# Strassen's method for the first product of the first layer's last eight columns, in a kernel that runs attention and two feed-forward layers

## The chip, the cores and the metric

The kernel runs on one core of a Trainium2 chip. The metric is the device time of one execution in microseconds; the median of a few runs is compared. One execution was also profiled, and every row below is from that one.

## The reference, cut to what matters

```python
def _moe_ref(x, w_in, w_out):            # first layer
    h = x @ w_in
    g = np.maximum(h, 0.0) + np.log1p(np.exp(-np.abs(h)))      # softplus
    return g @ w_out

def _moe2_ref(x, w_in, w_out):           # second layer
    h = np.maximum(x @ w_in, 0.0)
    return h * h @ w_out

attn_out = _attn_ref(q, k, v)            # windowed attention plus block summaries
x = attn_out, as [1536 tokens, 512]
x = _moe_ref(x, moe_w_in, moe_w_out)     # w_in [512, 2048], w_out [2048, 512]
return _moe2_ref(x, moe2_w_in, moe2_w_out)
```

The weights come as 64-bit floats and are converted in the kernel. All else is float32.

## The kernel before, in words

**Arithmetic.** Each float32 operand of the two layers is split into a high and a low part, and a product is three matmuls: high by high, high by low, low by high. d_ff has 2048 units, worked on as 16 "columns" of 128.

**First layer.** Part A runs columns 0 to 3 on blocks of 256 tokens while the attention still produces tokens (`steps`, flag `A`). Part B runs columns 4 to 9 and then 10 to 15 on three blocks of 512 tokens each, 36 steps in all. A B step is 12 matmuls of 512 columns in `mlp_in` (L680), softplus and the split of the gate (L686, L687, L689), and 12 matmuls of 512 in `mlp_out` (L706). The outputs add up in four PSUM banks (`accp` is one tile of two banks) and go into `part` (L729).

**Second layer.** `second` takes two columns at a time (a pair) and two pairs of token blocks z of 768 tokens (2 x 384). Its first product is Strassen's method in Winograd's form: 7 products of 6 matmuls of 384 columns (L992) in place of 8. One pair with one z is a "quad"; there are 16. The sums of weight blocks are made on POOL (L921), the sums of token blocks on DVE (L885) and split on ACT and DVE (L876) in `prepare`. `gate` turns a block of the product into a gate: `keep` (ACT), `add` (L999), square (L1008), high part (ACT), low part (L1016). The second product is plain: 6 groups of 6 matmuls of 512 (L1063). On PE the products of one quad alternate with the output groups of the quad before.

**Weights.** A load (L620, L623) lands in one of the `raw` buffers (4 in part A, 3 in the second layer). Four passes make float32 of it: L630 (ACT), L635 (DVE), a scaling (L314, ACT), L635 (DVE). Then ACT copies the high part into a weight slot and POOL subtracts (L606, L935, L948). A raw buffer is held until that split is done, and the split waits until the slot is free. There are 9 slots.

**Order.** Every step is an operation in a planner (`Plan`) with engine, assumed duration, due time and dependencies. For each engine it fixes one order ahead of time: of the operations that its model finds ready, the one due first. On the chip each engine then works through its own list in order. `rel` keeps a load's conversion from starting more than HOLD = 100 us before it is due.

Of the kernel before, what the change touches and what calls it, by code (L numbers as in the profile page):

```python
# [22 lines left out]
PH = ((0, 4), (4, 10), (10, 16))  # L23
LAG = 2
QT = 15.44
FIRST = 12.72
LAG_A = 3
NW_A = 6
NW = 9
NRAW = 4  # L30
NG = 3
LEAD = 16.0
HOLD = 100.0
# [154 lines left out]
def kernel(  # L188
# [47 lines left out]
    ga = [[wr.tile([128, 512], F32R, name=f"g{i}{n}") for n in "hl"] for i in range(2)]  # L236
# [4 lines left out]
    ws = [slot(wr, i) for i in range(NW_A)]  # L241
# [4 lines left out]
    att = ExitStack()  # L246
# [39 lines left out]
    for L in (1,):  # L286
        for ph, (f0, f1) in enumerate(PH):
            A = L == 1 and ph == 0
            n = 256 if A else 512
            for t0 in range(0, NT, n):  # L290
                for f in range(f0, f1):
                    steps.append(dict(A=A, L=L, ph=ph, c=NF * (L - 1) + f, t0=t0, n=n, first=f == f0, last=f == f1 - 1,
                                      fin=ph == len(PH) - 1, lastblk=t0 + n == NT, g=len(steps)))
    T = 24.0
    due_c, due_b = {}, {}
    for st in steps:
        st["T"] = T
        due_c.setdefault(st["c"], T)
        if st["A"]:
            due_b.setdefault(st["t0"] // 256, T)  # L300
        T += 24 * 0.2267 * st["n"] / 512 + (13.0 / PH[0][1] if st["A"] and st["t0"] < 1024 else 0.0)

    def due_t(t):
        return due_b[t // 2] - LEAD - 13.0 + 6.5 * (t % 2)

    NA = sum(st["A"] for st in steps)

# [282 lines left out]
    def weight(c, which):  # L590
        f, wi, wo = c, w1_in, w1_out
        i, s = nwt[0] % NRAW, c % NW
        nwt[0] += 1
        due = due_c[c] + which * (4.0 if c < PH[0][1] else 8.0)
        dv, dl = due - DV, due - DL
        if c < EARLY:
# [3 lines left out]
        need = [] if s < NW_A else ["late places"]  # L600

# [3 lines left out]
           r=[RL] + need, w=[("w", s, kh)])  # L605
        op(("POOL", "DVE"), (1.4, 1.0), dv, lambda e: tt(e).tensor_tensor(  # L606
            out=ws[s][kl], in0=lo.bitcast(F32), in1=ws[s][kh].bitcast(F32), op=ALU.subtract),
            r=[RL, ("w", s, kh)] + need, w=[("w", s, kl)])
# [35 lines left out]
    g_t, tmp = [], []  # L644

    def places(st):

        i = st["g"] - NA
        if st["A"]:
            return i % 2, i % 4  # L650
        return i % 4, (i + 2) % NG

    def hview(st):
        return hb[places(st)[0]][:, 0:st["n"]]

    def gview(st):
        i = places(st)[1]
        if st["A"]:
            return [x[:, 256 * (i % 2):256 * (i % 2) + 256] for x in ga[i // 2]]
        return g_t[i]  # L660

    def gkeys(st):
        i = places(st)[1]
        return [("g", i // 2, i % 2)] if st["A"] else [("g", i, 0), ("g", i, 1)]

    def xkeys(st, n):
        return [(n, t) for t in range(st["t0"] // 128, (st["t0"] + st["n"]) // 128)]

    def mlp_in(st):
        due, n, s = st["T"], st["n"], st["c"] % NW  # L670
        bl, o = divmod(st["t0"], 512)
        H_ = ("h", places(st)[0])
        gk = [(*x, "h") for x in gkeys(st)], [(*x, "l") for x in gkeys(st)]
        need = [] if st["A"] else ["late places"]

        def mm(ks_):
            for kk in ks_:
# [5 lines left out]
        op("PE", 12 * (0.0105 + 0.2162 * f), due, lambda: mm(range(NK)),  # L683
           r=xkeys(st, "xh") + xkeys(st, "xl") + [("w", s, "ih"), ("w", s, "il")] + need, w=[H_])
        ta, tv = 0.2 + 0.4 * f, 0.14 + 0.55 * f
        op("ACT", ta, due, lambda: nc.scalar.activation(out=hview(st), in_=hview(st), func=AF.Softplus), w=[H_], tab="sp")  # L686
        op("ACT", ta, due, lambda: nc.scalar.activation(out=gview(st)[0], in_=hview(st), func=AF.Copy),  # L687
           r=[H_] + need, w=gk[0])
        op("DVE", tv, due, lambda: nc.vector.tensor_tensor(  # L689
            out=gview(st)[1], in0=hview(st), in1=gview(st)[0].bitcast(F32), op=ALU.subtract),  # L690
            r=[H_] + gk[0] + need, w=gk[1])

    def mlp_out(st, due, gap=0.0):
        n, s = st["n"], st["c"] % NW
        gk = [(*x, p) for x in gkeys(st) for p in "hl"]
        A = st["A"]

        def mm(ms):
            gh, gl = gview(st)
            oh, ol = ws[s]["oh"], ws[s]["ol"]  # L700
            prs = ((oh, gh), (ol, gh), (oh, gl))
            for m, c in [(m, c) for m in ms for c in range(3)] if A else [(m, c) for c in range(3) for m in ms]:
                sl = slice(128 * m, 128 * m + 128)
                o = acc[m // 2][:, 256 * (m % 2):256 * (m % 2) + 256] if A else acc[m]
                for a, b in (prs[c],):
                    nc.tensor.matmul(out=o, lhsT=a[:, sl], rhs=b,  # L706
                                     start=(st["first"] and c == 0 and not (A and m % 2)),
                                     stop=(st["last"] and c == 2 and not (A and m % 2 == 0)))
        for i in range(2):
            op("PE", 0.71 if A else 1.36, due + gap * i, lambda i=i: mm((2 * i, 2 * i + 1)),  # L710
               r=gk + [("w", s, "oh"), ("w", s, "ol")] + ([] if A else ["late places"]),
               w=[("acc", i)] if A else [("acc", 2 * i), ("acc", 2 * i + 1)])

    def evac(st, due):
        t0, n = st["t0"], st["n"]
        bl, o = divmod(t0, 512)
# [6 lines left out]
        for m in range(4):  # L723
            pt, k_ = part[bl][:, m], ("part", bl, m)
            if st["ph"] == 0:
                op("ACT", 0.6, due, lambda m=m, pt=pt: nc.scalar.activation(out=pt, in_=acc[m], func=AF.Copy),
                   r=[("acc", m)], w=[k_])
            else:
                op("DVE", 0.7, due, lambda m=m, pt=pt: nc.vector.tensor_tensor(out=pt, in0=acc[m], in1=pt, op=ALU.add),  # L729
                   r=[("acc", m)], w=[k_])  # L730
# [13 lines left out]
    def late_places():  # L744
# [4 lines left out]
        ws.extend(slot(wr2, i) for i in range(NW_A, NW))  # L749
        g_t.extend(ga)  # L750
        g_t.extend([wr2.tile([128, 512], F32R, name=f"g{i}{n}") for n in "hl"] for i in range(2, NG))
# [457 lines left out]
```

## Time and profile before

| what | us |
|---|---|
| median of 3 runs | 606.68 (605.65 to 607.19) |
| the profiled execution | 607.07 |
| its span in the trace | 605.4 |

The 1.67 us between the last two lie outside the traced program. In the page, "busy" of PE counts pipelined matmuls and overstates the work; the time from one matmul's start to the next one's is the safer measure. A chain of waits is followed back from the last instruction to what released each one.

### The profile page before, as it was taken

To read this page: it belongs to the slowest core of one execution; us is meant where nothing else is said; L and a number is where in the kernel's file an instruction comes from. 1 tells how busy PE (TensorE), PEld (TensorE's weight loads), DVE (VectorE), ACT (ScalarE), POOL (GpSimd) and SP (SyncE) were. 2 spreads that over 40 slices of the span, in tenths; PEclk is the share of its full clock that TensorE was granted. 3 is DMA by queue.
4 is the path that set the end of the run, shared out by engine and by line. 5 is a ranking of instruction groups with operands and counts; after the bars stand their busy time and mean duration, and the time that the engine had idled before them with its cause. 6 is when DMAs were issued, how large, how long until landed. Compare 5 with 4: busy or idle time off the path is not lost.

```text
span 605.4 us, 9947 instructions
## 1 busy us (share of the span) xinstructions
PE 586.3 (97%) x3905; PEld 512.6 (85%) x3905; DVE 396.6 (66%) x581; ACT 330.9 (55%) x599; POOL 247.6 (41%) x235
## 2 busy tenths in 40 slices
PE   8688999999999999999999999999999999999997
PEld 6577988999888888888888898899988888898896
DVE  4987999924665126350228389876868586877854
ACT  4776888865664226452135565685755454545330
POOL 5967697524651034530000451735616061615210
PEclk9998999999999999999999999999999999999999
DMA  8999732332542023120000421133212122222212
GB/s 274 244 283 222 178 86 54 87 93 83 169 140 74 0 71 104 57 83 2 0 1 0 140 69 36 66 109 100 74 54 73 50 71 69 70 69 70 97 43 104
DMA packets 67215, 55.56 MB, mean 92 GB/s; under 512 B 36448, under 2 KB 61024, under 8 KB 67168
## 3 DMA queue, kind: packets, MB, share of 16 engines
q1 hardware_dynamic: 67168, 54.93, 31.9%
q8 instruction: 30, 0.49, 0.4%
q14 instruction: 17, 0.14, 0.1%
HBM read 51.77 MB, written 3.15 MB: 91 GB/s over the span
## 4 chain that ended last, share of the span: by engine, by line
PE 76%; DVE 12%; DMA 5%; ACT 2%; POOL 1%; issue 1%; SPq 1%; ACTq 0%; POOLq 0%
PE h L680 19%; PE h L992 16%; PE accp L706 12%; PE acc L706 8%; PE h L1063 7%; PE acc L1063 7%; PE accp L1063 6%; DMA raw<-in_moe_w_in_dram 3%; DVE raw L635 2%; DMA vwin<-in_v_dram 2%; DVE sm L524 1%; DVE mx L538 1%; DVE s L507 1%; SPq L390 1%; PE ab L569 1%
## 5 line engine op out<-in xcount | busy, mean ns | idle before, releaser
L635 DVE SCALAR_TENSOR_TENSOR raw<-raw 128x512 uint32<-128x512 uint32 x144 | 118.0, 837 | 43.1 <-ACT raw L630 25.0
L680 PE MATMUL h<-x,wih 128*128 128x512 f32 (+1 forms) x480 | 125.4, 349 | 0.0
L680 PEld LDWEIGHTS h<-x,wih 128*128 128x128 f32 x480 | 83.7, 189 | 12.1 <-POOL raw L316 0.4
L686 ACT ACTIVATE h<-h 128x512 f32<-128x512 f32 (+1 forms) x60 | 29.8, 498 | 99.9 <-PE h L680 99.8
L680 PE MATMUL h<-x,wil 128*128 128x512 f32 (+1 forms) x240 | 83.1, 346 | 0.0
L630 ACT ACTIVATE raw<-raw 128x512 uint32<-128x512 uint16 x67 | 44.8, 671 | 18.4 <-DMA raw<-in_moe_w_in_dram 9.4
L948 POOL TENSOR_TENSOR wil<-raw,wih 128x512 fp32r<-128x512 f32 x10 | 14.6, 1457 | 87.8 <-ACT wih L314 72.0
L680 PEld LDWEIGHTS h<-x,wil 128*128 128x128 f32 x240 | 45.3, 189 | 5.5
L314 ACT ACTIVATE raw<-raw 128x512 f32<-128x512 f32 x57 | 38.2, 672 | 17.9 <-DVE raw L635 17.9
L935 POOL TENSOR_TENSOR wih<-raw,wih 128x512 fp32r<-128x512 f32 x10 | 14.9, 1489 | 77.1 <-ACT wih L314 77.1
L921 POOL TENSOR_TENSOR raw<-raw 128x256 f32<-128x256 f32 x30 | 28.3, 945 | 29.6 <-DVE raw L635 29.1
L992 PE MATMUL h<-x,wil 128*128 128x384 f32 x192 | 38.5, 336 | 0.0
L992 PEld LDWEIGHTS h<-x,wil 128*128 128x128 f32 x192 | 34.4, 188 | 2.7
L992 PE MATMUL h<-x,wih 128*128 128x384 f32 x192 | 35.9, 335 | 0.0
L992 PEld LDWEIGHTS h<-x,wih 128*128 128x128 f32 x192 | 33.8, 188 | 1.4
L689 DVE TENSOR_TENSOR g1l<-h,g1h 128x256 fp32r<-128x256 f32 (+1 forms) x24 | 13.2, 550 | 26.3 <-ACT g1h L687 26.2
L314 ACT ACTIVATE woh<-raw 128x512 fp32r<-128x512 f32 (+1 forms) x34 | 22.2, 654 | 14.1 <-DVE raw L1008 6.0
L999 DVE TENSOR_TENSOR t<-t,h 128x384 f32<-128x384 f32 x32 | 17.6, 550 | 18.0 <-ACT t L314 12.3
L992 PE MATMUL h<-x,woh 128*128 128x384 f32 x144 | 28.9, 335 | 0.0
L316 POOL TENSOR_SCALAR wih<-raw 128x512 fp32r<-128x512 f32 x10 | 7.4, 736 | 52.5 <-PE h L680 44.8
L544 POOL TENSOR_TENSOR s<-s,sm 128x960 f32<-128x960 f32 (+1 forms) x14 | 22.5, 1610 | 13.4 <-DVE sm L526 12.5
L314 ACT ACTIVATE t<-h 128x384 f32<-128x384 f32 x32 | 15.6, 487 | 21.8 <-PE h L992 21.8
(343 smaller groups left out, 1551.2 us busy)
## 6 DMA issues: line engine op xcount, KB each, us to landing
raw<-in_moe_w_in_dram SPq DMA_DIRECT2D x36, 512.0 KB, 4.0
raw<-in_moe_w_out_dram SPq DMA_DIRECT2D x36, 512.0 KB, 3.3
vwin<-in_v_dram SPq DMA_DIRECT2D x20, 192.0 KB, 5.6
part<-in_k_dram SPq DMA_DIRECT2D x12, 256.0 KB, 5.5
late<-in_v_dram SPq DMA_DIRECT2D x2, 1536.0 KB, 11.2
out_dram<-part SPq DMA_DIRECT2D x12, 256.0 KB, 2.0
part<-in_q_dram SPq DMA_DIRECT2D x10, 256.0 KB, 5.3
vwin<-in_v_dram SPq DMA_DIRECT2D x4, 160.0 KB, 5.1
```

The source lines that it names most:

```text
L314: nc.scalar.activation(out=out_, in_=in_, func=AF.Copy, **({} if mul is None else {"scale": mul}))
L544: op(("POOL", "DVE"), (1.8 * n + 0.1, 1.75 * n), due, lambda e, sv=sv, rv=rv, spread=spread: tt(e).tensor_tensor(out=sv, in0=sv, in1=sprea ...
L630: nc.scalar.activation(out=lo, in_=q4[:, :, 1], func=AF.Copy, scale=2.0 ** -13, bias=-4095.5 / 8192.0)
L635: nc.vector.scalar_tensor_tensor(out=lo, in0=hi, scalar=n, in1=lo, op0=how, op1=ALU.bitwise_or)
L680: nc.tensor.matmul(out=hview(st), lhsT=ws[s][wn][:, w_], rhs=xx[bl][:, kk, o:o + n], start=(kk == 0 and xx is xh and wn == "ih"), stop=(kk ...
L686: op("ACT", ta, due, lambda: nc.scalar.activation(out=hview(st), in_=hview(st), func=AF.Softplus), w=[H_], tab="sp")
L706: nc.tensor.matmul(out=o, lhsT=a[:, sl], rhs=b, start=(st["first"] and c == 0 and not (A and m % 2)), stop=(st["last"] and c == 2 and not ...
L921: op("POOL", 0.85, due - 5.0 + d, lambda: nc.gpsimd.tensor_tensor(out=to, in0=x, in1=y, op=o), r=r, w=w)
L935: op("POOL", 0.2 + 1.2 * n / 512, d, lambda o=o_, j=j, x=x: nc.gpsimd.tensor_tensor(out=o(4 + j), in0=x, in1=o(j).bitcast(F32), op=ALU.sub ...
L992: nc.tensor.matmul(out=bk(b), lhsT=ws[i][m][:, c], rhs=half((z, x, xp), kk), start=first and kk == 0 and n == 0, stop=kk == 1 and n == 2, ...
L999: op("DVE", 0.58, URG, lambda: nc.vector.tensor_tensor(out=tmp[to], in0=tmp[x], in1=bk(b), op=ALU.add), r=[kb_(b)] + ([kt(x)] if x != to e ...
L1063: nc.tensor.matmul(out=out_bank(j), lhsT=x[:, cs], rhs=y, start=first and u == 0 and n == 0, stop=last and u == 1 and n == 2)
```

## The change

The first layer's columns 8 to 15 (four pairs) leave part B and become quads, in front of those of the second layer. Part B keeps columns 4 to 7 and runs its blocks in the order 1, 0, 2. `second` becomes `units`: 8 quads of the first layer and 16 of the second in one list. For every two pairs a and a+1 the order is (a, z=0), (a+1, z=0), (a+1, z=1), (a, z=1), so that the weights of both stay for both z; each pair is loaded once, where before two pairs of the second layer were loaded twice. `spot` gives a pair one of two sets of slots; there are 6 slots in place of 9.

New functions: `first_x` makes the token sums for the first layer out of the split x in three buffers `xt`, on DVE and ACT, once for each z; `second_x` is `prepare` with other places, and for z=1 its differences may go to POOL. `first_out` is the first layer's second product: 8 groups of 6 matmuls that alternate widths 512 and 256. For the first layer's quads the gate uses softplus on ACT in place of the square. The first 128 tokens of each block of 512, in place of the last, form the fourth token block. HOLD goes from 100 to 50, and raw buffers are 3 from column 4 on.

```diff
-PH = ((0, 4), (4, 10), (10, 16))
-QT = 15.44
-NW_A = 6
-NW = 9
-HOLD = 100.0
+NCA, NCL = 4, 8
+ORDER = (1, 0, 2)
+QT = (15.6, 15.44)
+NW = 6
+HOLD = 50.0
...
+    for bl in ORDER:
+        for c in range(NCA, NCL):
+            steps.append(dict(A=False, c=c, t0=512 * bl, n=512, first=c == NCA, last=c == NCL - 1, g=len(steps) - NA))
...
-        i, s = nwt[0] % NRAW, c % NW
+        i, s = nwt[0] % (NRAW if c < NCA else NRAW - 1), c % NW
...
+        quads = []
+        for L, pairs in ((0, range(NCL // 2, NF // 2)), (1, range(NF // 2))):
+            for a in pairs[::2]:
+                quads += [(L, a, 0), (L, a + 1, 0), (L, a + 1, 1), (L, a, 1)]
+        spot = [(u + 1) // 2 % 2 for u in range(len(uses))]
-        W_IN, W_OUT = ((7, 8), (1, 2)), (0, 3)
+        W_IN, W_OUT = ((2, 3), (5, 0)), (4, 1)
...
+            def whole(n, i, due):
+                def fn():
+                    for (o, a), (_, b) in zip(piece(n, "h", part_of(i)), piece(n, "l", part_of(i))):
+                        nc.vector.tensor_tensor(out=o, in0=a.bitcast(F32), in1=b.bitcast(F32), op=ALU.add)
+                op("DVE", 0.9, due, fn, r=keys(n, "h") + keys(n, "l") + ["late places"], w=[("xt", i)])
+            def diff(to, a, b, due):
+                op("DVE", 0.9, due, lambda: nc.vector.tensor_tensor(out=xt[to], in0=xt[a], in1=xt[b], op=ALU.subtract),
...
+            def diff(to, a, b, due):                     # second_x
+                op(("DVE", "POOL") if z else "DVE", (0.9, 2.1) if z else 0.9, due, lambda e="DVE": tt(e).tensor_tensor(
...
+                if not L:
+                    op("ACT", 0.5, URG - (0.0 if psum is None else 10.0), lambda: act(AF.Softplus, tmp[y] if psum is None else bk(psum)),
+                       r=[] if psum is None else [kb_(psum), *r3], w=[kt(y)], tab="sp")
...
+        def first_out(q, T_, h):
...
+            for m in range(4):
+                def mm(m=m):
+                    oh, ol = (ws[W_OUT[x]][n] for n in (("ih", "il"), ("oh", "ol"))[h])
+                    two = [acc[m], hb[2 + m // 2][:, 256 * (m % 2):256 * (m % 2) + 256]]
+                    g = double(gat[q, h, 0])
...
+                    for c, (a, b) in enumerate(((oh, g[0]), (ol, g[0]), (oh, g[1]))):
...
+                        for i in range(2):
+                            nc.tensor.matmul(out=two[i], lhsT=a[:, 128 * m:128 * m + 128], rhs=b[i],
...
+                due = T_ + QT[0] * (0.14 + 0.42 * h + 0.1 * m)
+                op("PE", 1.04, due, mm, w=[("acc", m), ("h", 2 + m // 2)],
...
+                op("DVE", 0.7, due - 30.0, put, r=[("acc", m)], w=[("pp", z, m, 0)])
+                if m % 2:
+                    op("DVE", 0.8, due - 30.0, put2, r=[("h", 2 + m // 2)], w=[("pp", z, m - 1, 1), ("pp", z, m, 1)])
...
+            if group(q)[1]:
+                z = quads[q][2]
+                if q == max(p for p, y in enumerate(quads) if y[0] == 0 and y[2] == z):
+                    second_x(z, Tq[q + 1] - 6.0)
...
+        first_x(0, T0 - 60.0)
+        first_x(1, T0 - 20.0)
```

## Rows read from the trace of the kernel before

**Rows 1.** Busy time by stage: engines, granted clock, DMA share, GB/s.
```profile
core 0: us, PE busy (x) PEld busy (x) DVE busy (x) ACT busy (x) POOL busy (x), PEclk, DMA share, GB/s
57.00:104.50 47.50, 44.64 (x619) 41.02 (x617) 46.64 (x66) 40.12 (x67) 37.34 (x33) 1.00 0.51 121
104.50:147.00 42.50, 42.46 (x465) 41.34 (x466) 24.55 (x40) 30.13 (x54) 18.41 (x15) 1.00 0.30 83
...
210.00:343.30 133.30, 133.30 (x590) 110.42 (x589) 52.99 (x73) 54.24 (x93) 29.50 (x28) 1.00 0.15 48
```

**Rows 2.** Chain that ended last, in order of time: A's outputs, part B.
```profile
149.84 4.31 PE accp L706 x36
...
180.12 2.72 PE h L680 x12
...
185.56 2.72 PE h L680 x12
```

**Rows 3.** The same chain, second layer: quad starts, products and output groups.
```profile
356.19 2.08 PE h L992 x12
...
409.13 1.04 PE h L992 x6
410.17 1.39 PE acc L1063 x6
...
498.41 2.08 PE h L992 x12
...
593.45 2.73 PE accp L1063 x12
```

**Rows 4.** PE in order of time, where width 512 follows width 256.
```profile
153.99 0.63 PE L680 MATMUL h<-x,wih 128*128 128x512 f32 x2
154.46 0.39 PE L680 MATMUL h<-x,wil 128*128 128x512 f32 x1
```

**Rows 5.** The chain at a change of z in the second layer.
```profile
514.05 1.06 PE h L992 x6
...
518.05 0.61 DVE part L1075
...
530.11 2.08 PE h L992 x12
```

**Rows 6.** DVE from 57 to 104.5 us, by line and shape: weight passes.
```profile
L635 DVE SCALAR_TENSOR_TENSOR raw<-raw 128x512 uint32<-128x512 uint32 x10 | 11.0, 1097 | 0.0
...
L606 DVE TENSOR_TENSOR wol<-raw,woh 128x512 fp32r<-128x512 f32 x2 | 3.9, 1960 | 0.1
```

**Rows 7.** DVE in order of time, after a quad's last product.
```profile
417.51 0.56 DVE L999 TENSOR_TENSOR raw<-raw,h 128x384 f32<-128x384 f32 x1 [0.67 <-PE h L992]
...
419.59 1.60 DVE L1016 TENSOR_TENSOR wil<-raw,wih 128x384 fp32r<-128x384 f32 x1
```

**Rows 8.** Groups by shape, whole run: low parts and sums of tokens.
```profile
L876 DVE TENSOR_TENSOR x<-part,x 128x768 fp32r<-128x768 f32 x12 | 11.2, 951 | 5.0 <-ACT x L314 4.9
...
L885 DVE TENSOR_TENSOR part<-part 128x768 f32<-128x768 f32 x8 | 7.6, 950 | 0.0
```

**Rows 9.** Busy time in the second layer's second quad, columns as in rows 1.
```profile
356.20:371.90 15.70, 15.70 (x79) 13.94 (x79) 15.70 (x26) 10.22 (x20) 1.19 (x1) 1.00 0.20 64
```

**Rows 10.** Weight passes in the second layer, by line and shape.
```profile
L635 DVE SCALAR_TENSOR_TENSOR raw<-raw 128x512 uint32<-128x512 uint32 x64 | 46.2, 738 | 14.1 <-ACT raw L630 8.6 <-ACT raw L314 5.2
...
L921 POOL TENSOR_TENSOR raw<-raw 128x256 f32<-128x256 f32 x24 | 23.3, 970 | 24.1 <-DVE raw L635 23.7
...
L630 ACT ACTIVATE raw<-raw 128x512 uint32<-128x512 uint16 x31 | 20.6, 665 | 6.6 <-DMA raw<-in_moe_w_in_dram 6.1 <-POOL wih L935 0.2
...
L935 POOL TENSOR_TENSOR wil<-raw,wil 128x512 fp32r<-128x512 f32 x8 | 13.1, 1638 | 0.1
```

**Rows 11.** The page's DMA issues: count, size, median us to landing.
```profile
raw<-in_moe_w_in_dram SPq DMA_DIRECT2D x36, 512.0 KB, 4.0
```

**Rows 12.** The chain at a weight load on which the end waited.
```profile
468.67 5.89 DMA raw<-in_moe_w_in_dram
```

More of the change, by code (lines that the diff above doesn't have):

```diff
@@ L285 @@
     steps = []
[L286 to L293, printed above, removed]
+    for t0 in range(0, NT, 256):
+        for c in range(NCA):
+            steps.append(dict(A=True, c=c, t0=t0, n=256, first=c == 0, last=c == NCA - 1, g=len(steps)))
+    NA = len(steps)
+    for bl in ORDER:
+        for c in range(NCA, NCL):
+            steps.append(dict(A=False, c=c, t0=512 * bl, n=512, first=c == NCA, last=c == NCL - 1, g=len(steps) - NA))
     T = 24.0
@@ L723, in evac @@
         for m in range(4):
[L724 to L730, printed above, removed]
+            pt = part[bl][:, m]
+            op("DVE", 0.7, due, lambda m=m, pt=pt: nc.vector.tensor_tensor(out=pt, in0=acc[m], in1=pt, op=ALU.add),
+               r=[("acc", m)], w=[("part", bl, m)])
     op("POOL", 3.0, -90, consts, w=["id"])
@@ L880, in diff @@
-            def diff(to, a, b_, due):
-                def flat(n):
-                    v = V[n][0]
-                    return v if S[n][0] == 3 or 3 not in bs else v.rearrange("p k (b t) -> p k b t", b=3)
-                op("DVE", 0.9, due, lambda: nc.vector.tensor_tensor(
-                    out=flat(to), in0=flat(a), in1=flat(b_), op=ALU.subtract),
-                    r=[K[n] for n in (a, b_) if n != to], w=[K[to]])
-            split("B11", "B11", due)
-            split("B22", "B22", due + 0.3)
@@ L1019, in quad_in @@
-            r3 = ["raw3", "late places"]
-            def keep(x, b):
-                op("ACT", 0.5, URG, lambda: copy("ACT", tmp[x], bk(b)), r=[kb_(b), *r3], w=[kt(x)])
+                        for i, (wp, xp) in enumerate((("h", "h"), ("h", "l"), ("l", "h"))):
+                            s, m = t[ti + (4 if wp == "l" else 0)]
+                            nc.tensor.matmul(out=bk(b), lhsT=ws[s][m][:, c], rhs=place(z, n, xp)[:, kk],
+                                             start=first and kk == 0 and i == 0, stop=kk == 1 and i == 2, skip_group_check=True)
@@ new lines, in first_out, with second_out, mm @@
+            gfree.extend(gat[q, h, 0] // 2 * 2 + b for b in range(2))
+        def second_out(q, T_, h):
+            L, f, z = quads[q]
+            x = spot[uses.index((L, f))]
+            first, last = group(q)
+            for c in range(3):
+                j, blk = 3 * h + c, h
+                due = T_ + QT[1] / 7 * (j + 1.5)
+                def mm(j=j, c=c):
+                    w = ws[W_OUT[x]]
+                    for v in range(2):
+                        gh, gl = unit(gat[q, v, blk])
+                        oh, ol = (w[n] for n in (("ih", "il"), ("oh", "ol"))[v])
+                        cs = slice(128 * c, 128 * c + 128)
+                        for n, (a, b) in enumerate(((gh, oh), (gh, ol), (gl, oh))):
+                            nc.tensor.matmul(out=out_bank(j), lhsT=a[:, cs], rhs=b, start=first and v == 0 and n == 0,
+                                             stop=last and v == 1 and n == 2)
+                op("PE", 1.36, due, mm, w=[bank_key(j)], r=[("gg", gat[q, v, blk], p) for v in range(2) for p in "hl"]
+                   + [("wo", x, v, p) for v in range(2) for p in "hl"])
@@ L1097, in second @@
+        first_x(1, T0 - 20.0)
+        op("NONE", 0.0, 0.0, quad_places, w=["quad places", *[("xt", i) for i in range(3)]])
         for q in range(len(quads)):
@@ L1140 @@
     stB = [st for st in steps if not st["A"]]
[L1141 removed]
+    nA = NCA
     blocks = 0
[L1143 to L1144 removed]
     def shrink():
@@ L1162 @@
     op("NONE", 0.0, 0.0, late_places, w=["late places"] + keys)
-    wq[nw[0]:nw[0]] = [(c, w, 0) for c, w, _ in late_w]
+    for i in range(2):
+        lock(("gates 0", 1 + i), [("g", 2 * i + j, p) for j in range(2) for p in "hl"])
     run_steps(stB, LAG)
```

547 lines of the change are left out of this document (300 added, 247 removed).

## The prediction, made before the result

> **What bounds the kernel now.** Read the stages first [rows 1]. From 104.5 us on PE is full: 42.46 of 42.50 us, then 133.30 of 133.30 us in the body of part B, with DVE, ACT and POOL all below half there. From 57 to 104.5 us two engines are nearly full: DVE 46.64 of 47.50, PE 44.64. Then read the chain of waits. In part B it is PE alone, one step every 5.44 us [rows 2]. In the second layer a quad takes 15.64 us when nothing disturbs it (498.41 to 514.05) [rows 3, 5]: 7 products of 1.04 and 6 output groups of 1.39. The 15 quads from 356.19 to 593.45 took 237.26 us, 2.66 more than 15 x 15.64 = 234.6 [rows 3]. So the reader should look for matmul columns, and for what disturbs quads; spare time on the other engines is worth nothing by itself.
>
> **PE's work.** Removed: 24 of 36 B steps, 24 x 5.44 = 130.6 us. Added: 8 quads. One stands for three steps (768 tokens by two columns), so 16.32 us.
> - Seven products: 7 x 1.04 = 7.28 us [rows 3].
> - Eight output groups of three matmuls of 512 and three of 256. A 512 costs 2.72/12 = 0.227 us, a 256 4.31/36 = 0.120 us [rows 2]; a group is 1.04 us, eight are 8.31.
> - The alternation itself isn't in the trace. Where widths grow there is a small fee: six matmuls of 512 among themselves take 1.36 us (half of 2.72) [rows 2], between products of 384 they take 1.39 [rows 3], so 0.03 for one change. Where 512 follows 256, the first two take 0.47 us up to the third's start, in place of 0.453 [rows 4], about 0.01 a matmul. A group changes upward three times. Bounds: 0, and three full fees, 0.09. I take 0.01 a time, 0.03 a group, since the fee in the trace is spread over several matmuls and here only one is long before the width falls again.
>
> Quad: 7.28 + 8.31 + 0.24 = 15.83 us, 0.49 less than 16.32. Eight quads: **-3.9 us**; bounds -5.8 (no fee) and -0.1 (full fee). The smaller matmuls eat half of what an eighth fewer product columns gives: the quad has 90 matmuls where three steps have 72, and beyond its columns each costs about 0.013 us (0.120 against 256 columns at the full 2.4 GHz, 0.107; granted clock 1.00) [rows 1, 2].
>
> Each of the 0.120 us matmuls has its own weight load, which is evidently hidden [rows 2]. The Trainium skill ("TensorE: Matmul & The Clock Gate", Part 3, The mechanism) says that a weight load overlaps running matmuls only where the row groups differ, and its LDWEIGHTS section gives 128 columns about 107 ns: 18 more matmuls would then cost 1.9 us a quad and the term would be about +7.7 us, an estimate. The row speaks against that rule here; it gets 1 in 100, within "slower" below.
>
> **The head.** Between 57 and 104.5 us DVE spends 11.0 + 3.9 us on weights [rows 6], most of it for columns 4 and 5, which part B needs only at 147. With HOLD 50 their passes start about 50 us ahead, near 97 us. DVE is full there, so the attention's chain gets shorter; but PE has only 47.50 - 44.64 = 2.86 us of idle time to give back [rows 1]. I take **-2.0**, bounds -2.9 and 0 (if other waits take the place). Eight passes at 1.1 us move behind 97 us, where DVE has 18 us free up to 147 and PE is full [rows 1]; that hides them.
>
> **Other work costed at nothing.** `first_x` is 10 sums, 8 differences and 8 low parts, all on 768 elements like those of [rows 8], 26 x 0.95, about 25 us of DVE in 65 us of part B; the old part B used 53 of 133 [rows 1]. If it were not done at the first quad, the first `keep` waits, since its buffers lie where `xt` was. Loads fall from 72 to 64. Start and end of the quads (two pending output steps; last groups, evacuation, stores) keep their form.
>
> **New waits.**
> - *Group ends in the first layer.* When z changes, banks are evacuated and PE waits: 514.05 to 530.11 is 16.06 us, 0.42 more than a quad, with the DVE evacuation just before PE goes on [rows 5]. `accp` is one tile for two banks, and `first_out` fills its second half right after the first. Four more such changes: **+1.7**, bounds 0 and 3.4 (a second wait at the shared h bank). The second layer has 8 groups before and after: its 2.66 us stays.
> - *The gate that comes last is needed first.* `first_out` with h=0 needs both halves of the first gate, and U2 is made after product 6. From its add to the end of its low part took 417.51 to 421.19, 3.68 us, with a weight pass and a slow subtraction in it [rows 7]. Cover: one group and two products, 3.12 us, and the low part is read only by the third pair of a group, 0.69 later: 3.81. **+0.4** in all; bounds 0 and 4.5 (one more pass of 0.69 in every quad, 0.56 uncovered each).
> - *Token sums of z=1 for the second layer.* 7 low parts and 4 differences, 11 x 0.95 = 10.5 us of DVE [rows 8]. Before, three z=0 quads covered it; DVE was full for a quad and PE lost nothing [rows 9]. Now two z=0 quads are there, and the first one still ends the outputs. B11 is needed first, T4 five products later. **+0.6**, bounds 0 and 3.8 (the four differences uncovered).
> - *Weights of a pair's second use.* With three raw buffers its second load follows the first half of the previous use's output weights, which wait until the output groups leave the slot. On SP the next output weights queue behind that load. Worked out from that end: split 0.67 + 1.64; landing 4.0 to 5.9; four passes 2 x 0.665 + 2 x 0.738 = 2.8; four sums at 0.97; split 0.67 + 1.64 [rows 10, 11, 12]. Total 15.3 to 17.2 us; S2 is read a quad, two products and a group later, 19.1. Before, the distance was two quads more. This happens at second-layer quads 5, 9 and 13 (from 0); in the first layer half a slot leaves sooner. **+0.5**, bounds 0 and 6 (each 2 us too late).
>
> **Sum.** -3.9 - 2.0 + 1.7 + 0.4 + 0.6 + 0.5 = -2.7 us. The profiled execution took 607.07 (span 605.4), so it would be 604.4 (602.7); it lay 0.39 above the median, and against 606.68 the forecast is **604.0 us**, 0.45% faster.
>
> **Rivals.**
> - *Better (600.5).* No fee for the widths (-5.8) and half the new waits (+1.6): -6.2. For it: the fee seen is only 0.01 a matmul [rows 4]. Against it: a change of z cost 0.42 us where the chain shows one [rows 5]. 0.15.
> - *Full fee (607.8).* Each growth of width costs 0.03: PE's term is -0.1, the total +1.1. For it: 0.03 is what one change costs in every output group [rows 3]. 0.12.
> - *No gain in the head (606.0).* Other waits, on POOL (37.34 of 47.50) or ACT (40.12) [rows 1], replace DVE's: +2.0 on the forecast. 0.12.
> - *Slower (610.0): the weight chain.* In-order ACT and DVE put gates between the four passes, and S2 comes 2 us late at each of the three places: +6.0. It passes 608.5 once each is over 1.5 us late. For it: DVE was full for a whole quad [rows 9], and a landing of 5.89 us stood on the chain [rows 12]. Against it: a slack of 1.9 to 3.8 us. With late gates and the rule above: 0.16.
> - *The forecast.* 0.45, own range 601.5 to 605.5.
>
> **Numbers.** A measurement tells this kernel from no change beyond about 0.3%: below 604.9, above 608.5. Faster: 0.42 of the forecast's 0.45 + 0.15 = 0.57. Same: 0.03 + 0.12 + 0.12 = 0.27. Slower: 0.16. The range for 8 in 10 is 599.5 to 609.0: it leaves out the best corner of "better" and the worse half of "slower".
>
> **What would show each step.** Part B: 12 steps at 5.44. First-layer quads: 15.83 from start to start, groups of six near 1.07; 1.04 or 1.13 tells the fee. 57 to 104.5: L635 nearly gone from DVE, PE's idle time below 1 us. At z changes of the first layer PE behind an evacuation. At the sixth second-layer quad PE waiting for POOL's L935 or for a weight load: then the weight chain has won. What would make me wrong most: a PE wait of several us at the start of the first layer's quads or of z=1's first second-layer quad.

## The result, and the profile after

The changed kernel takes 610.05 us (median of 4 runs, 609.61 to 610.48), the kernel before 606.16 us (median of 4 runs made beside them, 605.11 to 607.19). The ratio is 1.0064, 95% interval 1.0043 to 1.0085: slower, where the forecast was 604.0 us. The profiled execution of the changed kernel took 609.61 us, its span is 607.9 us; against the span of before, 605.4 us, that is 2.5 us more. The traces explain these 2.5 us; the medians lie 3.9 us apart because the profiled execution of before was 0.9 us above its median and that of after 0.4 us below.

Read the stages first, in the windows of [rows 1], with one more at the start of part B (columns as there).

```profile
57.00:104.50 47.50, 46.27 (x658) 43.11 (x657) 38.90 (x61) 38.57 (x63) 31.42 (x28) 1.00 0.42 95
104.50:147.00 42.50, 40.36 (x430) 38.86 (x419) 39.80 (x51) 32.82 (x63) 24.12 (x18) 1.00 0.32 94
130.00:150.00 20.00, 19.27 (x172) 18.45 (x172) 18.40 (x23) 13.23 (x30) 8.60 (x6) 1.00 0.17 54
```

PE gained 46.27 - 44.64 = 1.63 us of work in the first stretch, where 2.0 were forecast, with DVE down from 46.64 to 38.90. It lost 42.46 - 40.36 = 2.10 us in the second, where DVE went up from 24.55 to 39.80 [rows 1]. What left the first stretch came up in the second, and more: of the 15.25 us there, about 6 are weight passes (12 in place of 7) and 11 are the work of `first_x`, and there are about 2 us less of the rest.

Next, the alternation of widths, which no trace of before had. The chain of waits inside a first-layer quad:

```profile
230.42 0.23 PE acc L1111
230.64 0.12 PE h L1111
230.76 0.23 PE acc L1111
230.99 0.12 PE h L1111
231.11 0.23 PE acc L1111
231.34 0.12 PE h L1111
231.46 1.04 PE h L1022 x6
```

A group of three 512s and three 256s takes 231.46 - 230.42 = 1.04 us. There is no fee for the width at all.

Then the waits of PE from 210 to 605 us, the stretch of all quads: engine, line, what it waited for, total us, times, longest.

```profile
PE h L1022 <- DVE edge L1031: 1.8, 1, 1.8
PE accp L1151 <- DVE part L1163: 1.7, 2, 1.1
PE accp L1111 <- DVE part L1124: 1.3, 1, 1.3
PE h L1022 <- DVE raw L1052: 1.1, 1, 1.1
PE accp L1151 <- ACT part L310: 0.6, 1, 0.6
PE h L1022 <- DVE raw L1031: 0.5, 1, 0.5
```

Two kinds stand in this list and no third. PE waits to write `accp` until its evacuation has run (L1163, L1124, the ACT copy into `part`): the wait of [rows 5]. And PE's products wait for an `h` bank until DVE has read it (L1031, L1052). None names a weight, a load or POOL directly. The list leaves out waits under 0.15 us and counts the others from the modelled end of a matmul, so its 7.0 us are less than PE lost. From one matmul's start to the next, PE lost 11.2 us between quads in this trace: 5.5 at `accp`, at six places, and 5.7 at an `h` bank.

For the sizes, the starts of each quad's first product were taken from the trace. An undisturbed first-layer quad takes 15.60 us, a second-layer one 15.64, the first two together 28.48 (the last outputs of part B stand among them), and from the last quad's first product to the last matmul it is 23.97 in every trace. What a stretch took beyond that is a stall. Quads 8 to 11 are the second layer's first four; z=1 is first used by quad 10. For the kernel before, the second layer's sixteen quads are meant, the first four of them in the column of 8 to 11. The rows below the second are the experiments of the next section.

| kernel | ratio to before (95%) | first product, us | stalls of quads 0 to 7 | 8 to 11 | 12 to 23 | all stalls |
|---|---|---|---|---|---|---|
| before | 1 | 343.16 | none there | 0.10 | 2.56 | 2.66 |
| after | 1.0064 (1.0043 to 1.0085) | 212.18 | 1.96 | 4.61 | 4.77 | 11.34 |
| e1, differences on DVE | 1.0029 (1.0014 to 1.0044) | 212.53 | 1.96 | 3.13 | 4.20 | 9.28 |
| e2, HOLD 100 | 1.0186 (1.0165 to 1.0206) | 221.06 | 1.96 | 4.70 | 4.44 | 11.09 |
| e3, two tiles | 0.9977 (0.9964 to 0.9989) | 210.90 | 0.38 | 5.70 | 1.05 | 7.14 |
| e4, no DVE weight passes | 1.0028 (1.0010 to 1.0046) | 213.70 | 0.31 | 5.96 | 3.39 | 9.67 |
| e5, e1 and e3 | 0.9940 (0.9928 to 0.9951) | 212.31 | 0.38 | 2.97 | 0.93 | 4.28 |
| e6, before with two tiles | 0.9966 (0.9952 to 0.9981) | 342.59 | none there | 0.10 | 0.11 | 0.21 |
| e7, later due time | 1.0069 (1.0056 to 1.0082) | 212.52 | 1.91 | 4.64 | 5.02 | 11.58 |
| e8, e5 and e7 | 0.9946 (0.9930 to 0.9962) | 213.03 | 0.40 | 3.04 | 1.04 | 4.48 |
| e9, e5 and sums held | 0.9918 (0.9902 to 0.9934) | 210.19 | 0.42 | 3.03 | 0.53 | 3.98 |
| e10, e5 and z=1 earlier | 0.9913 (0.9896 to 0.9931) | 210.87 | 0.42 | 1.78 | 0.74 | 2.94 |
| e11, e5, e9 and e10 | 0.9902 (0.9884 to 0.9920) | 210.49 | 0.42 | 1.61 | 0.95 | 2.98 |

The sum for after: the first product begins 212.18 - (343.16 - 24 x 5.44) = -0.42 us away from where the old part B would put it; eight quads at 15.60 in place of 16.32 are -5.76; stalls are 11.34 - 2.66 = +8.68. Together +2.50 us, the difference of the spans.

### The profile page after: what moved, and what is told of

The parts are those of the page before. It is cut to its first block, busy times and chain, and to the rows that moved or that the text cites. A ratio compares the mean times of both kernels' runs of the same rounds, so it can differ in the third digit from the quotient of the medians.

```text
span 607.9 us, 10298 instructions
## 1 busy us (share of the span) xinstructions
PE 583.8 (96%) x4049; PEld 521.9 (86%) x4049; DVE 433.4 (71%) x639; ACT 347.4 (57%) x643; POOL 249.5 (41%) x233
## 4 chain that ended last, share of the span: by engine, by line
PE 65%; DVE 15%; DMA 6%; POOL 5%; ACT 5%; issue 3%; SPq 1%; ACTq 0%; DVEq 0%; POOLq 0%
PE h L1022 22%; PE acc L1151 6%; PE h L664 6%; PE h L1151 6%; PE accp L1151 5%; PE accp L684 5%; DMA raw<-in_moe_w_in_dram 3%; PE accp L1111 3%; DVE raw L629 3%; PE h L1111 3%; PE acc L684 3%; PE acc L1111 3%; DMA late<-in_v_dram 2%; POOL raw L952 2%; DVE x L824 2%
## 5 line engine op out<-in xcount | busy, mean ns | idle before, releaser
L629 DVE SCALAR_TENSOR_TENSOR raw<-raw 128x512 uint32<-128x512 uint32 x128 | 101.8, 814 | 24.4 <-ACT raw L624 12.3
L664 PE MATMUL h<-x,wih 128*128 128x256 f32 (+1 forms) x288 | 66.2, 322 | 0.7 <-DVE g L671 0.7
L1022 PE MATMUL h<-x,woh 128*128 128x384 f32 x288 | 57.9, 335 | 1.8 <-DVE edge L1031 1.8
L684 PE MATMUL accp<-g,woh 128*128 128x256 f32 (+1 forms) x240 | 54.8, 310 | 1.0 <-ACT part L696 0.9
L1022 PEld LDWEIGHTS h<-x,woh 128*128 128x128 f32 x288 | 50.4, 188 | 5.5 <-DVE edge L1031 2.2
L1022 PEld LDWEIGHTS h<-x,wil 128*128 128x128 f32 x288 | 50.5, 188 | 4.4 <-ACT t L310 1.2
L977 POOL TENSOR_TENSOR wil<-raw,wih 128x512 fp32r<-128x512 f32 x12 | 17.9, 1488 | 72.4 <-ACT wih L310 69.7
L664 PE MATMUL h<-x,wil 128*128 128x256 f32 (+1 forms) x144 | 45.9, 319 | 0.8 <-POOL wil L600 0.8
L684 PEld LDWEIGHTS accp<-g,woh 128*128 128x128 f32 x240 | 40.4, 190 | 4.3 <-ACT part L696 1.9
L1058 DVE TENSOR_TENSOR g<-raw,g 128x384 fp32r<-128x384 f32 x48 | 34.9, 731 | 12.5 <-ACT g L310 12.3
L310 ACT ACTIVATE g<-raw 128x384 fp32r<-128x384 f32 x48 | 24.9, 523 | 18.9 <-DVE raw L1055 14.8
L977 POOL TENSOR_TENSOR wol<-raw,woh 128x512 fp32r<-128x512 f32 x12 | 17.0, 1416 | 44.9 <-ACT woh L310 44.9
L684 PE MATMUL accp<-g,wol 128*128 128x256 f32 (+1 forms) x120 | 34.5, 304 | 0.0
L1031 DVE TENSOR_TENSOR raw<-raw,h 128x384 f32<-128x384 f32 x32 | 17.6, 551 | 18.8 <-ACT raw L310 16.5
```

What stands on the lines that cost most here:

```text
L310: nc.scalar.activation(out=out_, in_=in_, func=AF.Copy, **({} if mul is None else {"scale": mul}))
L629: nc.vector.scalar_tensor_tensor(out=lo, in0=hi, scalar=n, in1=lo, op0=how, op1=ALU.bitwise_or)
L664: nc.tensor.matmul(out=hview(st), lhsT=ws[s][wn][:, w_], rhs=xx[bl][:, kk, o:o + n], start=(kk == 0 and xx is xh and wn == "ih"), stop=(kk ...
L684: nc.tensor.matmul(out=o, lhsT=a[:, 128 * m:128 * m + 128], rhs=b, start=(st["first"] and c == 0 and not (A and m % 2)), stop=(st["last"] ...
L977: op("POOL", 1.4, due - 10.0, lambda o_h=o_h, o_l=o_l, lo=lo: nc.gpsimd.tensor_tensor(out=o_l, in0=lo.bitcast(F32), in1=o_h.bitcast(F32), ...
L1022: nc.tensor.matmul(out=bk(b), lhsT=ws[s][m][:, c], rhs=place(z, n, xp)[:, kk], start=first and kk == 0 and i == 0, stop=kk == 1 and i == 2 ...
```

## The experiments

All start from the changed kernel unless another is named.

**e1: the differences of z=1 on DVE.** The planner could put the differences of the second layer's z=1 tokens on POOL, and did. Here it can't.

```
-                op(("DVE", "POOL") if z else "DVE", (0.9, 2.1) if z else 0.9, due, lambda e="DVE": tt(e).tensor_tensor(
+                op("DVE", 0.9, due, lambda e="DVE": tt(e).tensor_tensor(
```

> Edit: the four token differences of z=1 for the second layer go to DVE alone, none to POOL. Theory (POOL work holds DVE up: in the trace of the changed kernel four differences of 2.2 us on POOL stand beside low parts that take 2.6 and 3.5/2 us in place of 0.95, and PE loses 4.2 us over the tenth and eleventh quad): about 4 x 0.95 us more on DVE but no stretched operations, PE loses 1 us or less there, 606 to 607.5 us. Rival (DVE is simply over-full there, whoever makes the differences): no gain or up to 2 us slower, 609.5 to 612 us.

It ran at 1.0029 of before, 608.12 us, about 0.35% better than after. That is more than the theory's range and less than the rival's. Stalls fell by 2.06 us, 1.48 of them in quads 8 to 11. What POOL's differences did is seen in after, with DVE and POOL in order of time (start, us, engine, line, operation):

```profile
360.29 3.48 DVE L824 TENSOR_TENSOR x<-part,x 128x768 fp32r<-128x768 f32 x2
363.69 0.68 DVE L629 SCALAR_TENSOR_TENSOR raw<-raw 128x512 uint32<-128x512 uint32 x1
364.30 2.59 DVE L824 TENSOR_TENSOR x<-part,x 128x768 fp32r<-128x768 f32 x1
366.81 0.54 DVE L1031 TENSOR_TENSOR edge<-edge,h 128x384 f32<-128x384 f32 x1
...
357.77 4.32 POOL L918 TENSOR_TENSOR part<-part 128x768 f32<-128x768 f32 x2 [4.56 <-DVE x L824]
363.92 2.16 POOL L918 TENSOR_TENSOR part<-part 128x768 f32<-128x768 f32 x1 [1.83 <-DVE x L824]
366.04 2.01 POOL L977 TENSOR_TENSOR wol<-raw,woh 128x512 fp32r<-128x512 f32 x1
```

A difference takes 2.16 us on POOL, and the DVE low part that meets it takes 2.59 where it needs 0.95 [rows 8]. PE's longest wait, 1.81 us, ends with the add at 366.81 that stood behind them. In e1 the groups of DVE from 336 to 372 us are undisturbed (mean ns after the comma):

```profile
L824 DVE TENSOR_TENSOR x<-part,x 128x768 fp32r<-128x768 f32 x6 | 5.5, 952 | 0.2 <-ACT x L310 0.2
L918 DVE TENSOR_TENSOR part<-part 128x768 f32<-128x768 f32 x4 | 3.8, 952 | 0.0
```

In after, five of these low parts took 8.0 us there, 1.6 each. So the differences cost about 2 us, but 3.13 us of stall stayed in these quads, where the theory left 1 us or less: they are one cause of several.

**e2: weight passes as early as before.**

```
-HOLD = 50.0
+HOLD = 100.0
```

> Edit: HOLD back to 100, so that the weights of columns 4 to 7 are again converted up to 100 us ahead. Theory (HOLD 50 only moved these passes from the stretch of 57 to 105 us into 100 to 150 us, where PE then waited; the head gained 0.4 us in all): PE's idle time moves back to 57 to 105 us, the start of the first quad stays within 1 us of 212.2, 609.5 to 611 us. Rival (the late passes are what costs, and the head would have given 2 us with a better place): the first quad starts 1.5 to 2.5 us earlier.

618.08 us, 1.0186 of before, which neither side had foreseen. The quads are as in after, 11.09 us of stalls; the first product begins at 221.06, 8.9 us later. From 85 to 110 us PE is busy for 20.02 of 25 us (after: 24.05):

```profile
85.00:110.00 25.00, 20.02 (x288) 18.22 (x288) 23.01 (x27) 16.43 (x27) 19.12 (x16) 0.93 0.34 91
```

and between 57 and 130 us DVE's weight passes take 22.8 us, 16 of them, against 15.3, 13 of them, in after. PE's longest wait there, 2.4 us up to 92.1 us, is for the attention's tokens on DVE (L575), and from 92.0 to 95.3 us the granted clock is 0.51, the lower of the two levels of 1.2 and 2.4 GHz. Over the stretch its mean is 0.93, beside PE's idle time of 5 us; in after it is 1.00. So with the new order of weights the shorter lead keeps the head whole, and a longer one gives the quads nothing.

**e3: two banks, two tiles.** `accp` is one tile over two banks; here each bank is its own tile, as the other two `acc` banks are. Nothing is computed otherwise.

```
-    acc_pair = ps_m.tile([128, 2, 512], F32, name="accp")
-    acc = [acc_pair[:, m] for m in range(2)]
+    acc = [ps_m.tile([128, 512], F32, name=f"accp{m}") for m in range(2)]
...
-        scb, sck = (acc_pair, "acc") if t == 1 else (sc, "sc")
+        scb, sck = (acc[0:2], "acc") if t == 1 else ([sc[:, hh] for hh in range(2)], "sc")
```

> Edit: the two PSUM banks that were one tile become two tiles; nothing else is changed, but the planned orders may move. Theory (at each change of z PE waits for the evacuation of the first bank before it may write the second, only because both are one tile; 10 to 11 changes at 0.4 to 0.9 us): 3 to 6 us less, 604 to 607 us, no PE wait on an evacuation left. Rival (the wait is for the bank's own evacuation or for DVE's queue, which comes anyway a group later): less than 1 us, 609 to 610.5 us.

604.92 us, 0.9977 of before. The place where it shows is the fifth quad of after. PE and DVE there, in order of time (in brackets the idle time before, and its end):

```profile
281.21 1.21 PE L1022 MATMUL h<-x,woh 128*128 128x384 f32 x6
283.74 0.50 PE L1111 MATMUL accp<-g,woh 128*128 128x512 f32 x1 [1.32 <-DVE part L1124]
...
282.10 0.98 DVE L629 SCALAR_TENSOR_TENSOR raw<-raw 128x512 uint32<-128x512 uint32 x1 [0.75 <-ACT raw L310]
283.00 0.68 DVE L1124 TENSOR_TENSOR part<-accp,part 128x512 f32<-128x512 f32 x1
284.98 0.69 DVE L1124 TENSOR_TENSOR part<-accp,part 128x512 f32<-128x512 f32 x1 [1.29 <-PE accp L1111]
```

The first bank's evacuation stands on DVE behind a weight pass and ends at 283.68; PE, which wants the second bank, begins at 283.74. The same place with two tiles:

```profile
279.94 1.20 PE L1021 MATMUL h<-x,woh 128*128 128x384 f32 x6
280.98 0.39 PE L1110 MATMUL accp<-g,woh 128*128 128x512 f32 x1
...
280.81 0.99 DVE L628 SCALAR_TENSOR_TENSOR raw<-raw 128x512 uint32<-128x512 uint32 x1 [0.74 <-ACT raw L309]
281.72 1.27 DVE L1123 TENSOR_TENSOR part<-accp,part 128x512 f32<-128x512 f32 x2
```

The weight pass is as late, the evacuation as late, and PE writes the second bank 0.74 us before the evacuation of the first begins. Stalls of quads 0 to 7 fall by 1.58 us and those of 12 to 23 by 3.72. The first product comes 1.28 us earlier too, at the same granted clock of 0.95 from 20 to 57 us: in after PE waits 0.9 us of the head behind the evacuations of the head's own blocks (L696), and that wait is no longer listed. In quads 8 to 11 the stalls grow by 1.1. PE waits 2.34 us there for the add that in after cost 1.81, and then runs at the clock's lower level, as PE's rows and the row of the stretch (columns as in [rows 1]) show:

```profile
365.66 1.60 PE L1021 MATMUL h<-x,woh 128*128 128x384 f32 x6 [2.34 <-DVE edge L1030]
367.49 0.63 PE L1150 MATMUL h<-wil,g 128*128 128x512 f32 x1
367.91 0.63 PE L1150 MATMUL h<-wih,g 128*128 128x512 f32 x1
...
366.70:369.95 3.25, 3.25 (x10) 2.48 (x9) 3.25 (x4) 1.66 (x4) 1.84 (x1) 0.51 0.50 161
```

Matmuls of 512 columns start 0.42 to 0.43 us apart here, in place of 0.227, and that costs about 1.6 of the 5.70 us; after the wait of 1.81 us in the changed kernel the granted clock stayed at 1.00. All that is listed of PE's waits from 210 to 602 us is now this:

```profile
PE h L1021 <- DVE edge L1030: 2.3, 1, 2.3
PE h L1021 <- DVE raw L1030: 0.3, 1, 0.3
PE h L1021 <- ACT raw L309: 0.2, 1, 0.2
```

**e4: the quads' weights without their two DVE passes.**

```
-        op("DVE", 0.75 if own else 0.95, dv, lambda: join(ALU.bitwise_and, 0x80000000), r=[RH], w=[RL])
+        if not own:
+            op("DVE", 0.95, dv, lambda: join(ALU.bitwise_and, 0x80000000), r=[RH], w=[RL])
...
```

and likewise for the second `join`. 

> Edit: for the quads' weights the two DVE passes of each load are left out (48 loads, 96 passes of 0.74 us, 71 us of DVE), so the weights are wrong; all the rest stays. Theory (DVE's own list is what the quads' waits go through: evacuations and gates stand behind weight passes that wait for a load): of the 11.4 us that PE loses between quads 3 us or less are left, 601 to 603 us. Rival (the chain of slot, load and POOL sums sets it): 2 us less at most, 607.5 to 609.5 us.

608.36 us, 1.0028: the theory failed, and the time lies in the rival's range. With nearly 70 us less on DVE (361.8 of the first 600 us, after 430.6) the stalls of quads 0 to 7 and 12 to 23 fall by 1.65 and 1.38 us, those of quads 8 to 11 rise by 1.35. These hold one wait of 2.8 us for a gate on DVE, and behind it a stretch at the lower clock (granted clock 0.53 from 373.2 to 376.6 us) that costs about 1.6 us. The rival's own chain isn't shown either: the waits that are listed name evacuations and gates, and no weight or POOL sum. So the passes seem a burden where evacuations stand behind them, which e3 removes without leaving work out. The head's first product is 1.5 us later here; from 20 to 57 us the mean granted clock was 0.86 where after had 0.95, so that part isn't read as an effect of the edit.

**e5: e1 and e3 together.** 

> Two earlier edits together: the two accumulator banks as two tiles, and the differences of the second layer's tokens of z=1 on VectorE alone. Theory (two separate causes: the product's banks behind one tile cost 5.1 us between the quads, the differences on GpSimd cost 1.6 us between the tenth quad of the run and the thirteenth): the gains add; the stretch of three quads before 402 us falls from 52.1 us with two tiles alone to 49 to 50 us, and the time to 601.5 to 603.5 us, 0.992 to 0.995 of the kernel before. Rival (with two tiles VectorE is the bound of 342 to 371 us anyway, and the differences lengthen its list by what they shorten its operations): the time stays at 604.5 to 605.5 us, as with two tiles alone.

602.68 us, 0.9940. The stretch of three quads before the thirteenth took 400.3 - 350.7 = 49.6 us (after: 51.1, e3: 52.1, e1: 49.6), inside the theory's 49 to 50. In this order, 11.34 us of stalls, less 2.06 (differences on DVE), less 5.00 (two tiles, from e1 to e5), leaves 4.28. The two don't simply add up: alone, the tiles took off 4.20 (e3), 0.80 less than here. The 1.6 us at the lower clock, which e3 has and e5 doesn't, are more than enough for that. Of the 4.28, 0.93 us are in quads 12 to 23, all of it in quads 13, 17 and 21 (15.85, 16.17 and 15.83 us; every other one 15.64): the second layer's sixth, tenth and fourteenth. The chain of waits at the tenth, and ACT and PE there in order of time:

```profile
480.85 1.60 POOL wil L976
482.46 0.02 issue
482.47 4.56 DMA raw<-in_moe_w_in_dram
...
487.11 0.69 ACT L623 ACTIVATE raw<-raw 128x512 uint32<-128x512 uint16 x1 [0.42 <-DMA raw<-in_moe_w_in_dram]
487.71 0.67 ACT L309 ACTIVATE raw<-raw 128x512 f32<-128x512 f32 x1
488.26 0.65 ACT L309 ACTIVATE woh<-raw 128x512 fp32r<-128x512 f32 x1
488.82 0.66 ACT L309 ACTIVATE raw<-raw 128x512 f32<-128x512 f32 x1
489.37 0.48 ACT L309 ACTIVATE raw<-h 128x384 f32<-128x384 f32 x1
...
489.90 1.31 PE L1021 MATMUL h<-x,wol 128*128 128x384 f32 x6
```

A weight load waits for its raw buffer, which POOL's low part frees, and lands 4.56 us later; four ACT passes on weights follow; and the copy that frees PE's `h` bank stands behind them. It is the weight chain, and it holds PE up through ACT's order, not by weights that are missing. This place and a like one in quad 13 make about 0.56 of the 0.93 us. The rest, 0.2 us each, stands at 482.26 and 545.35 us, where ACT's copy is late behind a gate's DVE operation. That takes 1.67 us in place of 0.56 while POOL splits a weight:

```profile
479.60 1.67 DVE L1054 SCALAR_TENSOR_TENSOR edge<-edge 128x384 f32<-128x384 f32 x1
479.23 1.63 POOL L962 TENSOR_TENSOR woh<-raw,woh 128x512 fp32r<-128x512 f32 x1
```

**e6: the kernel before with two tiles.** The edit of e3 in the kernel before. 

> The kernel before, with its two banks of one tile made two tiles, and nothing else. Theory (the tile orders the evacuations only where products wait for accp, and before did so at 2.7 us of stalls in all between its quads): 0.4 to 2 us shorter, 604.2 to 605.8 us, so that the changed kernel with two tiles is worth about nothing against it. Rival (the kernel before has slack there, and its planner gives another order at the head too): within 0.3% of before or longer, 606 to 608 us, so that the fix belongs to the change alone.

604.07 us, 0.9966, 0.13 us under the theory's range. Its sixteen quads have 0.21 us of stalls left of 2.66. So most of the 2.66 us of [rows 3] was the tile too: 2.0 of it stand at `accp` in the trace of before, at five places of 0.4 us. Compared tile for tile, e3 against e6, 0.9977 against 0.9966 with intervals that overlap, the change does nothing measurable; it begins to pay with the differences on DVE (e5, 0.9940, whose interval ends just below that of e6).

**e7: a later due time for the first layer's sums.**

```
-        first_x(0, T0 - 60.0)
+        first_x(0, T0 - 40.0)
```

> The changed kernel, with the sums and differences of the first layer's tokens of z=0 held back in the planner's time until part B has begun. Theory (those sums stand before the gates on VectorE between 134 and 150 us, and PE waits 0.7 us there for a gate; with the weight passes held up by them, they gave back most of the head's gain): PE idle between 130 and 150 us falls from 0.7 us to under 0.2 us, and the first product begins 0.5 to 1 us earlier, at 211.2 to 211.7 us; time 609 to 609.6 us. Rival (VectorE is so full from 130 to 250 us that what is held back is late at the first products or pushes the weight passes): the first product's quad or the third begins later, 611 to 614 us.

The text on record speaks of sums kept back until part B runs, but the kernel under this label had only the later due time. The planner starts what is ready when an engine is free, and left nearly all the sums where they were: PE is busy for 19.27 of 130 to 150 us, as in after. So it tests neither side. At 1.0069 against 1.0064 it shows something smaller: a few operations changed in order are worth less than a measurement can tell. e9 is the test.

**e8: e5 with that due time.** 

> Two tiles, the differences of z=1 on VectorE, and a later due time (by 20 us, which moves few operations) for the sums of the first layer's tokens of z=0. Theory (gains add, the due time does little): 601.5 to 603.5 us, within 0.2% of the kernel with the two edits alone. Rival (each change of a due time turns over the planner's order and costs or gives 1 to 2 us wherever it lands): it differs from the kernel with the two edits by over 0.3%.

0.9946 against 0.9940 for e5, as the theory had it, within the intervals. So this one turn of the planner's order cost nothing measurable; that holds for this edit, and isn't shown for others.

**e9: the sums really held.** e5, with a release time for the sums of z=0.

```
-                op("DVE", 0.9, due, fn, r=keys(n, "h") + keys(n, "l") + ["late places"], w=[("xt", i)])
+                op("DVE", 0.9, due, fn, r=keys(n, "h") + keys(n, "l") + ["late places"], w=[("xt", i)], rel=0.0 if z else T0 - 40.0)
```

> Two tiles and the differences on VectorE, as in the kernel with both, and the sums of the first layer's tokens of z=0 kept from starting until part B runs (a release time in the planner, which moves them behind the first four gates of part B; a later due time alone had left them where they were). Theory (those sums stand before the gates between 134 and 150 us, and PE loses 0.7 us there): PE idle of 130 to 150 us falls from 0.73 us to under 0.2 us, nothing is late later, and the time is 0.4 to 0.8 us under that of the kernel with both, 601.9 to 602.3 us. Rival (what is held back is then late at the first products or pushes the weight passes behind it): the first four quads take 0.5 us or more longer, or begin no earlier, and the time is 602.6 to 604 us.

601.51 us, 0.9918, a little under the theory's range. In after the gates at the start of part B stood on DVE behind `xt` (chain of waits: L858 and L862 end, then L671 runs, and PE with it):

```profile
142.11 1.24 DVE xt L858
143.35 0.75 issue
144.10 0.41 DVE g L671
```

Held back, DVE has 5.67 us of work from 130 to 150 us in place of 18.40, and PE is full:

```profile
130.00:150.00 20.00, 20.00 (x179) 19.31 (x179) 5.67 (x11) 10.84 (x26) 5.90 (x6) 1.00 0.17 54
```

The first product begins at 210.19 (e5: 212.31, with the clock of 20 to 57 us at 0.91 and 0.86), and the quads have no more stalls than in e5. Of these 2.12 us, 0.96 are there before the held sums matter: the attention's last matmul begins at 132.75 us (e5: 133.71). The other 1.2 us come behind it, 0.73 of them as idle time in this window, and only these can be put down to the edit.

**e10: z=1's preparation earlier.** e5, with the due time of the second layer's z=1 preparation put 54 us earlier, ahead of gates and weight passes.

```
-                    second_x(z, Tq[q + 1] - 6.0)
+                    second_x(z, Tq[q + 1] - (6.0, 60.0)[z])
```

> As the kernel with two tiles and the differences on VectorE, and the preparation of the second layer's tokens of z=1 due 54 us earlier, so that on VectorE it goes before the gates and weight passes of the two quads around it. Theory (2.7 us of PE's waits between 366 and 378 us are left because that preparation is interleaved with weight passes and gates, although VectorE has 4 us idle between 336 and 372 us): the three quads before 400 us fall from 49.6 us to 47.0 to 48.5 us, and the time by 1 to 2.5 us, to 600.2 to 601.7 us. Rival (VectorE has too much work between the last evacuation of z=1 and the eleventh quad, so that the gates which are passed are late in their turn): 49 us or more, 602.4 to 604 us.

601.11 us, 0.9913, in the theory's range. The stalls of quads 8 to 11 fall from 2.97 to 1.78 us. DVE now has no idle time from 352 to 372 us, and PE still loses 0.60:

```profile
352.00:372.00 20.00, 19.40 (x99) 17.26 (x98) 20.00 (x35) 13.15 (x23) 0.00 (x0) 1.00 0.10 32
```

So both sides were partly right: the order was worth 1.2 us, and DVE has no free time there for more. The one wait that is listed there, 0.6 us, is for an ACT copy out of an `h` bank, so it isn't shown that DVE makes up what is left.

**e11: both.** 

> Both edits of the order, on two tiles and with the differences on VectorE. Theory (each acts in its own stretch): the sum of what the two runs beside it give, 599.6 to 601.3 us, 0.989 to 0.992 of the kernel before. Rival (the order that the planner makes of both turns over elsewhere): no better than the better of the two.

600.22 us, 0.9902 (0.9884 to 0.9920): the lowest median, in the theory's range, 1.6% under the changed kernel as it was given and 0.6% under e6, the best form of the kernel before that was run. Its interval overlaps those of e9 and e10, and its stalls are those of e10, so the rival, no better than the better of the two, isn't ruled out.

## Why the prediction was wrong, point by point

The forecast had -2.7 us; the profiled spans give +2.5. The 5.2 us between them, term by term:

- **PE's work: right in kind, too small.** Forecast -3.9 with a fee of 0.01 a matmul; measured -5.76, the end of the range without a fee. The small loss in [rows 4] was not a property of changing widths within a group. 1.9 us better than forecast. The rule of the Trainium skill ("TensorE: Matmul & The Clock Gate", Part 3, The mechanism) that by the prediction's estimate would have made this term about +7.7 us doesn't hold here: the group of 1.04 us above has six weight loads, none of them visible.
- **The head: wrong.** Forecast -2.0, measured -0.42. The step that failed is "Eight passes at 1.1 us move behind 97 us, where DVE has 18 us free up to 147 and PE is full [rows 1]; that hides them." The first half came (PE's idle time from 57 to 104.5 us fell from 2.86 to 1.23, DVE by 7.7 us), but the free time was given out twice. `first_x`, costed at nothing in part B, starts once the attention's places are free, ahead of part B's gates; between 104.5 and 147 us DVE had 39.80 us of work, not 24.55 plus eight passes. And evacuations of `accp` stood in PE's way here too. e9 took back 0.73 us of idle time by holding those sums, e3 1.28 by the two tiles; with both, the first product comes at 210.2 to 210.5 us (e9, e11), 2.1 to 2.4 us ahead of the old place, about what was forecast. The waits of PE that are left there are the attention's own. 1.6 us worse.
- **Group ends: near in sum, not place by place.** Forecast +1.7 with the old 2.66 staying, 4.4 in all; e1 against e5 shows 5.0 us for the one tile. The prediction named the cause and counted four places in the first layer at 0.42. After's trace has one place there, at 1.6 us, with a late weight pass ahead of the evacuation on DVE; that one reaches the forecast of four is chance. In the second layer the waits at `accp` rose from 2.0 to 3.9 us, where nothing was to change. 0.6 us worse.
- **Token sums of z=1 for the second layer: the term that decided.** Forecast +0.6, bounds 0 and 3.8; measured 5.0: 2.06 that e1 removed and 2.97 that e5 still has in quads 8 to 11. The step that failed is "11 x 0.95 = 10.5 us of DVE". Four differences ran on POOL at 2.16, and DVE's operations beside them stretched to 1.6 us and more. And the cover was worse than two z=0 quads: low parts, weight passes, gates and the last first-layer evacuations keep DVE busy for 18.77 of the 20 us from 352 to 372. Before, a quad with DVE full [rows 9] cost PE nothing; that three quads stood between is the likely reason, but no run tests it. 4.4 us worse, outside its bounds. Counted in after's trace alone, the three waits of quads 9 and 10 (they end at 367.41, 371.24 and 373.04 us) cost 4.2 us, outside its bounds as well.
- **The gate that comes last needed first: near by chance.** Forecast +0.4; quads 0 to 7 of e5 have 0.38 us of stalls in all. But no matmul of `first_out` starts late there: 0.3 of it stand in quad 7, where a product waits for an `h` bank that DVE's add is reading. So the term itself came out at nothing, and the 0.4 belongs to a wait that no term had.
- **Weights of a pair's second use: right place, somewhat small.** Forecast +0.5 at second-layer quads 5, 9 and 13, counted from 0; e5 shows 0.93 at just these. The step that differs is who waits: not the products for S2 but PE for an `h` bank that ACT was to free. As the rival "slower (610.0)" it would have had to cost 6 us; that the result came out at almost that number is chance, since the token sums and the head made it. 0.4 us worse.

Sum: -1.9 + 1.6 + 0.6 + 4.4 + 0.4 = +5.1. The split between the tile and the token sums depends by some tenths on the order in which the edits are counted. Of "what would show each step", the 5.44 us steps, the near empty weight passes of 57 to 104.5 us (L629 four times, 4.8 us, before ten, 11.0) and an evacuation at a change of z in the first layer (one of the four counted) came as written, and so did "a PE wait of several us" at z=1's first second-layer quad, named there as what would make the forecast most wrong. Groups took 1.04 us, not 1.07, and PE's idle time from 57 to 104.5 us was 1.23 us, not below 1.

## What to carry to other kernels

When a change takes work from the bounding engine, add up the second engine's work in each stretch that the moved pieces enter, all pieces together: here DVE's free time up to 147 us and around 350 us was counted for each piece alone, and around 350 us alone that cost most of the 5.76 us that PE gave back. If an accumulator spans two banks and is drained half by half, give each half its own tile, or PE waits for the other half's drain: worth 0.3% before and 0.9% after. And an alternative engine for an operation is costed with what it does to its neighbour, not by its own duration alone.

## What the runs showed of the hardware that was not expected

A VectorE operation with two inputs in SBUF waits while a GpSimd operation runs. The low part that starts at 364.30 us meets a POOL difference that runs until 363.92 + 2.16 = 366.08, and ends at 366.89, 0.81 us after it, about its own duration. The add at 366.81, with one input in PSUM, takes its usual 0.54 us although L977 runs on POOL until 368.05. The whole trace of after says the same: the weight pass L629, with both inputs in SBUF, takes 0.69 us in the median where POOL does nothing (77 of them, none over 0.70), and 1.11 where it begins during a POOL operation (32 of them, up to 2.28). The add L1031 takes 0.55 either way. The Trainium skill ("SBUF — State Buffer", Who interferes with whom) says that a VectorE instruction with two SBUF inputs contends with a GpSimd instruction that reads SBUF, over a pair of ports that is an exclusive lock; these rows agree. So each of the four differences on POOL could hold DVE up for as long as it ran.

Matmuls of 512 and 256 columns in turn, each with its own weights, cost 0.23 + 0.12 us a pair, with nothing for the change.
